# One engine for the output's copy, fewer maxima beside it, and a fourth maximum in an MLP's bursts: a transformer block on one core

## The chip, the core and the metric

The kernel runs on one core of a Trainium2 chip. The metric is the device time of one execution in microseconds (us). The core's engines are TensorE (PE; its weight loads are shown as PEld), VectorE (DVE), ScalarE (ACT), GpSimd (POOL) and SyncE (SP), which here issues every DMA. TensorE's results go to PSUM, of which there are eight banks of 128 x 512 fp32.

## The reference

```python
def _A_ref(x, wqkv, wo):                # S = 2048, D = 512
    H = 32; Dh = D // H                 # 32 heads of 16
    qkv = (x @ wqkv).reshape(B, S, 3, H, Dh).transpose(2, 0, 3, 1, 4)
    q, k, v = qkv[0], qkv[1], qkv[2]
    p = softmax(einsum("bhqd,bhkd->bhqk", q, k) * Dh ** -0.5)
    o = einsum("bhqk,bhkd->bhqd", p, v)
    return o.transpose(0, 2, 1, 3).reshape(B, S, D) @ wo

def _B_ref(x, w1, w2):                  # F = 1792
    return silu(x @ w1) @ w2

h = x + _A_ref(layernorm(x), wqkv, wo)
out = h + _B_ref(layernorm(h), w1, w2)
```

All is fp32; the weights of the MLP are scaled up by about 4.9.

## The kernel before

**Stages.** First the rows are normalized and projected to queries, keys and values. Then comes attention, in 32 *items*: an item is four heads for one block of 512 queries, so the eight items 8b to 8b+7 make up block b. An item has 16 *groups*, one for each 128 keys. Once the items of a block are done, its output projection is put beside groups 10 to 15 of the following item (`output`, in items 8, 16 and 24), and after that item the block's MLP runs (`finish_block`, `mlp`, at the group numbers in `marks`). Block 3 has its own ending (`finish_last`).

**A group** (main loop, numbers g; item i, group c): four score products (`scores`, tile `ps_s`, 64 rows of the array each), each followed on ScalarE by an exponential into `pt`; between them up to three maxima (`one_max`); and behind them the four value products of group g - 2 (`values`, tile `pv`, one bank for all items).

**Maxima.** The exponentials need each query's largest score beforehand. For that each item needs 64 *maxima* (`maximum`): a product of 48 rows into `ps_m`, on the other half of the array from the score before it, and a VectorE reduction of its 512 columns to `mx`. They are made ahead, for items up to four later. When the 64 of an item are complete, `finish_max` reduces them once more on VectorE and splits them on GpSimd (`ns`). Two steps later (`WAIT`) `place_max` transposes them on TensorE (`ps_n`), copies them (`mt`, on VectorE during attention) and places them by two DMAs into the query tile of their item. `maxima(g)` says how many a group gets, from a planner's rate with the maxima in the MLPs (`BESIDE`) taken off.

**Banks.** In attention and the MLPs one bank is `pv`, three (kind "sm") turn between maxima and their transposition, and four (kind "st") between scores, projections and the MLP's four sums `acc`.

**The end of an item.** After the values of its last group, which stand behind the scores of the next item's group 1, `finish_item` copies `pv` to `pvs`, the first half on ScalarE and the second on VectorE, and DMAs carry it on. The next item's values, behind group 2, overwrite `pv` and so come after both copies.

**An MLP** has 14 steps (`FC`). In each the first product (12 matmuls, into `pv`; in step 0 another bank) goes through `gate` (SiLU and a rounding on ScalarE, a subtraction `gl` on VectorE), and then the step before's second product (`second`, 12 matmuls to `ps_acc`) follows. `weave` puts bursts of three maxima behind the matmuls of given numbers: 4 and 12 of the first product and 8 of the second, or 4 and 10 of both in the steps of `EXTRA`. Each engine's instructions keep the order in which they are written down, since all are recorded with `keep_in_program_order`.

Of the kernel before, what the change touches and what calls it, by code (L numbers as in the profile page):

```python
# [10 lines left out]
F32 = mybir.dt.float32  # L11
# [9 lines left out]
P = 128  # L21
# [5 lines left out]
DC = D // P  # L27
FC = F // P
# [17 lines left out]
HEADS = [(0, 1), (0, 0), (1, 1), (1, 0)]  # L46
ITEMS = NB * H // 4

WAIT = 2
AHEAD = 4  # L50


BESIDE = (132, 132, 117)
OUTPUT = 9

BESIDE_A = (6,), 6

BESIDE_C = {3: ((4, 12), (8,)), 4: ((4, 10), (4, 10))}
BURST = 3

EXTRA = (4, 8), (6,), ()

QUIET = FC, FC, FC - 1


@with_exitstack
def attention_mlp_kernel(ctx: ExitStack, tc: tile.TileContext, x, wqkv, wo, w1, w2, out):
# [59 lines left out]
    def bank(name, kind="st", dtype=F32):  # L127
        return banks[kind].tile([P, 512], dtype, tag=kind, name=name)
# [73 lines left out]

    mx, left = {}, {}

    def maximum(i, kb, qt, a, j):
# [4 lines left out]
        ps = bank("ps_m", "sm")  # L210
        mm(ps, qs[i % RING][64 * j:64 * j + 48, a, qt * P:qt * P + P],
           ks[i % RING][64 * j:64 * j + 48, a, kb * 512:kb * 512 + 512], start=True, stop=True)
        pin(nc.vector.tensor_reduce(mx[i][:, j, a, qt, kb:kb + 1], ps, axis=AX.X, op=ALU.max))  # L213
        left[i] -= 1
        return left[i] == 0
# [34 lines left out]
    at = {"item": 0, "done": 0, "half": 0, "step": 0, "due": 0, "attention": False}  # L250
    agenda = {}

    def soon(steps, fn, *a):
# [10 lines left out]
            at["item"] += 1  # L264
        return at["item"]

    def one_max(half=None):
# [9 lines left out]
        if maximum(*todo[i, half].pop(0)):  # L277
            soon(WAIT, place_max, i, finish_max(i))

    def burst(n):  # L280
        for _ in range(n):
            one_max()

    def weave(steps, places, n=BURST):

        for k, _ in enumerate(steps):
            if k + 1 in places:
                burst(n)


    with ExitStack() as pa:
# [53 lines left out]
        def project_qk(b, n, beside=((), 0), scale=False):  # L345
# [4 lines left out]
            weave(product(ps, lambda c: wqk_h[:, c, cols], lambda c: wqk_l[:, c, cols],  # L350
                          lambda c: xth[b][:, c, :], lambda c: xtl[b][:, c, :], DC), *beside)
# [93 lines left out]
        for g in range(1, NG // 2):  # L445
            for m, (b, key) in enumerate([(b, 1) for b in range(NB)] + [(b, 0) for b in range(NB)]):
                tick()
                if g == 1 and m < 2:
                    fixed_rows(2 + m)

                n = 8 * g + m - 12
                project_qk(b, 2 * g + key, BESIDE_A if n < 19 else ((), 0), True)
# [16 lines left out]
    groups = ITEMS * KC  # L469
    pts, den = {}, {}  # L470

    def scores(g, k):

        i, c = divmod(g, KC)
        a, j = HEADS[k]
        assert i in placed
        ps = bank("ps_s")
# [20 lines left out]
    def finish_item(i):  # L498

        b, u = divmod(i, 8)  # L500
        pvs = bp.tile([P, 512], F32, name="pvs", bufs=1)
        act("copy", pvs[:, :256], pv[:, :256])
        dve("tensor_copy", pvs[:, 256:], pv[:, 256:])
        if i == ITEMS - 1:
            last.append(pvs)
            return
        dma(dn[i], pvs.rearrange("(k r) n -> k r n", r=32)[:, DH, :])
        for k in range(4):
            dma(ot[b % 2][place(i, k), :, u // 2, :], pvs[32 * k:32 * k + 16, :].rearrange("d (t n) -> d t n", n=P))
# [103 lines left out]
        low(gl, g, gh)  # L613
        return gh, gl

    def second(b, acc, f, gh, gl, places):
        w2h, w2l = ws.pop(("w2", f))
        while f == 0 and len(acc) < 4:
            acc.append(bank("ps_acc"))
        steps = (product(acc[t], lambda c: gh[:, t * P:(t + 1) * P], lambda c: gl[:, t * P:(t + 1) * P],  # L620
                         lambda c: w2h, lambda c: w2l, 1, start=f == 0, stop=f == FC - 1) for t in range(4))
        if f < FC - 1:
            weave(chain.from_iterable(steps), places)
            return
        for t, step in enumerate(steps):
            run(step)
            n = 4 * b + t
            h = rows_of(b, t)
            dve("tensor_tensor", h, acc[t], h, ALU.add)
            dma(out[n * P:(n + 1) * P, :], h)  # L630

    def mlp(b):

        first = bank("ps_w1")
        acc = [bank("ps_acc") for _ in range(3)]
        waiting = None
        for f in range(FC):
            tick()
# [9 lines left out]
            weave(product(ps, lambda c: w1h[:, c, :], lambda c: w1l[:, c, :],  # L648
                          lambda c: hth[:, c, :], lambda c: htl[:, c, :], DC), places[0])
            parts = gate(ps)  # L650
            if waiting:
                second(b, acc, *waiting, places[1])
# [35 lines left out]
    def finish_last(pending):  # L688
# [94 lines left out]
        for f in range(FC):  # L783
# [11 lines left out]
            if f:  # L795
                split_weights("w2", f - 1, "dve")
            if f > 1:
                second(b, acc, *waiting.pop(0), ())
        split_weights("w2", FC - 1, "dve")
        while waiting:  # L800
            second(b, acc, *waiting.pop(0), ())

    marks = [KC * (8 * b + 1) for b in range(1, NB)]

    def maxima(g):
# [18 lines left out]
    for g in range(groups):  # L824
        tick()
        i, c = divmod(g, KC)
        if g in marks:
# [7 lines left out]
        if i in (8, 16, 24):  # L835
            b, n = i // 8 - 1, c - OUTPUT
            if c < 4:
                load_rows(b, c)
# [14 lines left out]
                    soon(5, split_weights, "w1", f, "dve", "dve")  # L853
        if g == 1:
            dve("memset", pv, 0.0)
        n = maxima(g)
# [5 lines left out]
        if i in (8, 16, 24) and c > OUTPUT:  # L862
# [37 lines left out]
```

## Time and profile before

| | |
|---|---|
| median of 3 runs | 1729.4 us (1729.32 to 1729.89) |
| the profiled execution's own time | 1728.78 us |
| its span | 1727.0 us |
| TensorE busy | 1683.9 us (98%) |
| VectorE busy | 1460.4 us (85%) |
| ScalarE busy | 1247.6 us (72%) |
| granted TensorE clock, mean | 0.994 |

The span runs from the first to the last instruction that was recorded, and the execution's own time is 1.8 us longer. Matmuls are pipelined, so that a busy TensorE is not one at its peak, and TensorE's waits are read from the starts of its instructions. In the timeline each row has the start (us), the length (us), the engine, the line, the operation, output and input tiles with their shapes and the count of merged instructions; in brackets the idle time before it and what ended it. In the waits each row has who waited for whom, the total (us), how often, and the longest. In the table by stretches the columns are the stretch, its length, busy time and count of PE, PEld, DVE, ACT and POOL, the granted TensorE clock, the DMA share and GB/s. In the page's groups: line, engine, operation, tiles and shapes, count, busy time (us), mean of one (ns), idle time before them and what ended it.

### The profile page before, as it was taken

How to read it: one execution, taken by the hardware profiler on the slowest of the kernel's cores; microseconds unless marked ns; L12 is line 12 of the kernel's file. 1: busy time of each engine (PE TensorE's matmuls, PEld its weight loads, DVE VectorE, ACT ScalarE, POOL GpSimd, SP SyncE). 2: the span in 40 equal slices, each digit the busy share in tenths (PEclk: the TensorE clock that was granted, in tenths of full speed). 3: DMA queues.
4: the chain of work that ended last, by engine and by line, in shares of the span. 5: the costliest groups of instructions: out<-in, count | busy, mean ns of one | idle time of the engine just before them, and what ended most of it. 6: DMA issues, size and time to landing. Idle time of an engine off the chain costs nothing.

```text
span 1727.0 us, 28338 instructions
## 1 busy us (share of the span) xinstructions
PE 1683.9 (98%) x10498; PEld 648.1 (38%) x10498; DVE 1460.4 (85%) x2459; ACT 1247.6 (72%) x2465; POOL 233.0 (13%) x318
## 2 busy tenths in 40 slices
PE   6999999999999999999999999999999999999999
PEld 5656422222245532222245542222235542222377
DVE  6899899999978889999978889999978789997343
ACT  5223599999963269999963359999973369999743
POOL 2113300000032310000033310000023310000000
PEclk9999999999999999999999999999999999999999
DMA  6334311121222111111222211111122211100122
GB/s 186 101 80 152 112 35 37 36 48 38 62 70 77 56 48 31 36 42 44 59 59 79 67 40 32 40 38 44 53 70 80 68 34 45 34 11 20 56 80 80
DMA packets 100570, 102.81 MB, mean 60 GB/s; under 512 B 19028, under 2 KB 77204, under 8 KB 100432
## 3 DMA queue, kind: packets, MB, share of 16 engines
q1 hardware_dynamic: 100432, 101.01, 19.8%
q8 instruction: 82, 1.34, 0.3%
q14 instruction: 56, 0.46, 0.1%
HBM read 77.72 MB, written 17.29 MB: 55 GB/s over the span
## 4 chain that ended last, share of the span: by engine, by line
PE 58%; ACT 35%; DVE 4%; DMA 2%; issue 1%; SPq 0%; ACTq 0%; POOL 0%; POOLq 0%; DVEq 0%
ACT pt L88 33%; PE pv L74 19%; PE ps_acc L74 9%; PE ps_m L74 8%; PE ps_s L74 8%; PE ps_qk L74 5%; PE ps_wo L74 3%; PE ps_w L74 3%; DVE mx L213 2%; PE ps_v L74 2%; PE ps_tr L77 1%; DVE ot L91 1%; DMA va<-in_A_wqkv_dram 1%; DMA ks<-kd 1%; DVE pvs L91 1%
## 5 line engine op out<-in xcount | busy, mean ns | idle before, releaser
L213 DVE TENSOR_REDUCE mx<-ps_m 128x1 f32<-128x512 f32 x2048 | 1281.1, 682 | 108.5 <-PE ps_m L74 80.1
L88 ACT ACTIVATE pt<-ps_s 128x512 f32<-128x512 f32 x2048 | 1019.6, 616 | 41.1 <-PE ps_m L74 37.8
L74 PE MATMUL ps_s<-qs,ks 64*128 64x512 f16 x2048 | 550.6, 382 | 4.3 <-ACT pt L88 1.5
L74 PE MATMUL pv<-pt,va 128*17 128x512 f32 x4096 | 540.4, 601 | 6.3 <-DVE pvs L91 6.2
L74 PE MATMUL ps_m<-ks,qs 48*128 48x512 f16 x2048 | 527.7, 382 | 7.3 <-DVE mx L213 5.7
L74 PEld LDWEIGHTS <-ks 64*128 64x128 f16 x2048 | 153.9, 95 | 568.0 <-issue 458.3
L74 PEld LDWEIGHTS pv<-pt,va 128*17 128x17 f32 x4096 | 68.8, 95 | 233.8 <-issue 213.1
L74 PEld LDWEIGHTS <-qs 48*128 48x128 f16 x2048 | 122.8, 94 | 66.8 <-issue 63.1
L88 ACT CAST w2h<-w 128x512 fp32r<-128x512 f32 x56 | 34.7, 619 | 105.5 <-PE ps_acc L74 105.5
L88 ACT ACTIVATE g<-pv 128x512 f32<-128x512 f32 x39 | 23.3, 597 | 105.2 <-PE pv L74 105.2
L81 POOL TENSOR_SCALAR nm<-nm 128x16 f32<-128x16 f32 x32 | 8.3, 259 | 666.4 <-DVE nm L220 666.4
L74 PE MATMUL ps_acc<-w2h,gh 128*128 128x512 f32 x224 | 92.0, 411 | 0.0
L74 PE MATMUL ps_acc<-w2l,gh 128*128 128x512 f32 x224 | 91.3, 408 | 0.0
L74 PE MATMUL ps_acc<-w2h,gl 128*128 128x512 f32 x224 | 88.9, 397 | 0.0
L91 DVE TENSOR_TENSOR gl<-g,gh 128x512 fp32r<-128x512 f32 x56 | 40.2, 717 | 49.9 <-ACT gh L88 49.9
L81 POOL TENSOR_TENSOR w2l<-w,w2h 128x512 fp32r<-128x512 f32 x42 | 53.6, 1277 | 180.2 <-ACT w2h L88 180.2
L74 PE MATMUL pv<-hth,w1l 128*128 128x512 f32 x156 | 65.9, 423 | 0.0
L81 POOL TENSOR_TENSOR ot<-ot,den 128x512 f32<-128x512 f32 (+1 forms) x16 | 20.4, 1275 | 331.0 <-DMA den<-dr 292.8
L74 PE MATMUL pv<-hth,w1h 128*128 128x512 f32 x156 | 62.4, 400 | 0.0
L74 PE MATMUL pv<-htl,w1h 128*128 128x512 f32 x156 | 61.5, 394 | 0.0
L88 ACT ACTIVATE ks<-ps_qk,qk_s 128x512 f32<-128x512 f32 x24 | 16.5, 689 | 61.8 <-PE ps_qk L74 61.8
L81 POOL TENSOR_TENSOR w1l<-w,w1h 128x512 fp32r<-128x512 f32 x42 | 55.2, 1315 | 22.9 <-ACT w1h L88 22.9
(118 smaller groups left out, 1278.0 us busy)
## 6 DMA issues: line engine op xcount, KB each, us to landing
w<-in_B_w_dram SPq DMA_DIRECT2D x112, 256.0 KB
ks<-kd SPq DMA_DIRECT2D x120, 192.0 KB
qs<-qd SPq DMA_DIRECT2D x128, 48.0 KB
kd<-sh SPq DMA_DIRECT2D x16, 256.0 KB
qd<-sh SPq DMA_DIRECT2D x16, 256.0 KB
hx<-in_A_x_dram SPq DMA_DIRECT2D x16, 256.0 KB
out_dram<-ot SPq DMA_DIRECT2D x16, 256.0 KB
ot<-pvs SPq DMA_DIRECT2D x124, 32.0 KB
```

Of the source, the lines that this page charges most:

```text
L74: tc.keep_in_program_order(nc.tensor.matmul(*a, **k))
L77: tc.keep_in_program_order(nc.tensor.transpose(*a))
L81: tc.keep_in_program_order(getattr(nc.gpsimd, op)(*a, **k))
L88: pin(getattr(nc.scalar, fn)(*a, **k))
L91: pin(getattr(nc.vector, fn)(*a, **k))
L213: pin(nc.vector.tensor_reduce(mx[i][:, j, a, qt, kb:kb + 1], ps, axis=AX.X, op=ALU.max))
```

## The change

- The output's copy (`finish_item`) is no longer split. VectorE copies all of it; in items 8, 16 and 24, whose copy stands at the head of an MLP, ScalarE does; the last item keeps the halves.
- Group 2 of an item finds at most two maxima instead of three (`JOINT`, in `maxima`), save for items 0 to 2 and the items after an MLP.
- The transposition of an item's maxima is put off to the next group 2 (`due_at`), where that is early enough and no MLP has just run.
- In an MLP the burst in the second product (the second one in an `EXTRA` step) is of four; the first of these goes to `pv`. There are three, two and no `EXTRA` steps instead of two, one and none, and the third MLP's bursts end one step earlier (`QUIET`).
- Groups 10 to 13 of items 8, 16 and 24 find up to four maxima, with `BESIDE` counting 141, 138 and 112 in the MLPs.
- Eight scores of the two groups after an MLP are made inside its last two second products, in the banks of the maxima (`some_scores`), with the load of the exponential's table moved ahead; these two groups find no maxima instead of four each.
- Ahead of attention the last projection of queries and keys gets a burst of four.

```diff
-BESIDE = (132, 132, 117)
+BESIDE = (141, 138, 112)
...
-BESIDE_A = (6,), 6
-BESIDE_C = {3: ((4, 12), (8,)), 4: ((4, 10), (4, 10))}
-BURST = 3
-EXTRA = (4, 8), (6,), ()
-QUIET = FC, FC, FC - 1
+BESIDE_A = {6: 6}, {4: 4}
+BESIDE_C = ({4: 3, 12: 3}, {8: 4}), ({4: 3, 10: 3}, {4: 3, 10: 4})
+EXTRA = (4, 7, 10), (4, 8), ()
+QUIET = FC, FC, FC - 2
...
+    def due_at(i):
+        g = at["group"]
+        if g is None:
+            return WAIT
+        joint = g + WAIT + (JOINT - g - WAIT) % KC
+        return joint - g if joint < KC * i - 2 and joint // KC - 1 not in (-1, *FIRSTS) else WAIT
...
-            soon(WAIT, place_max, i, finish_max(i))
+            soon(due_at(i), place_max, i, finish_max(i))
...
-        act("copy", pvs[:, :256], pv[:, :256])
-        dve("tensor_copy", pvs[:, 256:], pv[:, 256:])
+        if i == ITEMS - 1:
+            act("copy", pvs[:, :256], pv[:, :256])
+            dve("tensor_copy", pvs[:, 256:], pv[:, 256:])
+        elif i in FIRSTS:
+            act("copy", pvs, pv)
+        else:
+            dve("tensor_copy", pvs, pv)
...
+        ahead = [(g, m ^ (g % 2)) for g in marks[b:b + 1] + [marks[b] + 1] for m in range(4)]
+        def some_scores(n):
+            for _ in range(n):
+                scores(*ahead.pop(0), "sm")
...
-            places = BESIDE_C[4 if f in EXTRA[b] else 3] if f < QUIET[b] else ((), ())
+            beside_1, beside_2 = BESIDE_C[f in EXTRA[b]] if f < QUIET[b] else ({}, {})
+            beside_1 = {k: (lambda n=n: burst(n)) for k, n in beside_1.items()}
+            beside_2 = {k: (lambda n=n: burst(n, *[pv] * (n == 4))) for k, n in beside_2.items()}
+            if f == FC - 1:
+                beside_2 = {8: lambda: some_scores(3)}
...
+            if f == FC - 1:
+                act("activation", small.tile([P, 1], F32, name="sw"), ident[:, :1], AF.Exp)
...
-        act("activation", small.tile([P, 1], F32, name="sw"), ident[:, :1], AF.Exp)
-        second(b, acc, *waiting, ())
+        second(b, acc, *waiting, {2: lambda: some_scores(3), 8: lambda: some_scores(2)})
...
-        if g < LAG + 3 or g in marks or g - 1 in marks:
-            at["due"] = 0
+        if g < LAG + 3:
+            at["due"] = 1
             return 4
-        n = max(0, min(3, int(at["due"]), ready - at["done"]))
+        if g in marks or g - 1 in marks:
+            return 0
+        most = 2 if c == JOINT and i > 2 and i - 1 not in FIRSTS else 4 if i in FIRSTS and OUTPUT < c < OUTPUT + 5 else 3
+        n = max(0, min(most, int(at["due"]), ready - at["done"]))
...
-            scores(g, k)
+            if (g, k) not in pts:
+                scores(g, k)
```

More of the change, by code (lines that the diff above doesn't have):

```diff
@@ L47 @@
 ITEMS = NB * H // 4
+FIRSTS = 8, 16, 24
 WAIT = 2
+JOINT = 2
 AHEAD = 4
-BESIDE = (132, 132, 117)
+BESIDE = (141, 138, 112)
 OUTPUT = 9
-BESIDE_A = (6,), 6
-BESIDE_C = {3: ((4, 12), (8,)), 4: ((4, 10), (4, 10))}
-BURST = 3
-EXTRA = (4, 8), (6,), ()
-QUIET = FC, FC, FC - 1
+BESIDE_A = {6: 6}, {4: 4}
+BESIDE_C = ({4: 3, 12: 3}, {8: 4}), ({4: 3, 10: 3}, {4: 3, 10: 4})
+EXTRA = (4, 7, 10), (4, 8), ()
+QUIET = FC, FC, FC - 2
 @with_exitstack
@@ L203, in attention_mlp_kernel, with maximum @@
     mx, left = {}, {}
-    def maximum(i, kb, qt, a, j):
+    def maximum(i, kb, qt, a, j, ps=None):
         if i not in mx:
@@ L209, in maximum @@
             left[i] = 64
-        ps = bank("ps_m", "sm")
+        if ps is None:
+            ps = bank("ps_m", "sm")
         mm(ps, qs[i % RING][64 * j:64 * j + 48, a, qt * P:qt * P + P],
@@ L249, in attention_mlp_kernel @@
     END = 64 * ITEMS
-    at = {"item": 0, "done": 0, "half": 0, "step": 0, "due": 0, "attention": False}
+    at = {"item": 0, "done": 0, "half": 0, "step": 0, "due": 0, "attention": False, "group": None}
     agenda = {}
@@ L265, in next_item, with one_max @@
         return at["item"]
-    def one_max(half=None):
+    def due_at(i):
[4 more added lines that the diff above has]
+        return joint - g if joint < KC * i - 2 and joint // KC - 1 not in (-1, *FIRSTS) else WAIT
+    def one_max(half=None, ps=None):
         i = next_item()
@@ L276, in one_max, with burst, weave @@
         at["done"] += 1
-        if maximum(*todo[i, half].pop(0)):
-            soon(WAIT, place_max, i, finish_max(i))
-    def burst(n):
-        for _ in range(n):
+        if maximum(*todo[i, half].pop(0), ps):
+            soon(due_at(i), place_max, i, finish_max(i))
+    def burst(n, *more):
+        for ps in more:
+            one_max(ps=ps)
+        for _ in range(n - len(more)):
             one_max()
-    def weave(steps, places, n=BURST):
+    def weave(steps, inserts):
         for k, _ in enumerate(steps):
-            if k + 1 in places:
-                burst(n)
+            if k + 1 in inserts:
+                inserts[k + 1]()
     with ExitStack() as pa:
@@ L343, in measure, with project_qk @@
             pin(nc.scalar.reg_load(qk_f, qk_e[:1, :].bitcast(U32)))
-        def project_qk(b, n, beside=((), 0), scale=False):
+        def project_qk(b, n, beside={}, scale=False):
             g, key = divmod(n, 2)
@@ L350, in project_qk @@
             weave(product(ps, lambda c: wqk_h[:, c, cols], lambda c: wqk_l[:, c, cols],
-                          lambda c: xth[b][:, c, :], lambda c: xtl[b][:, c, :], DC), *beside)
+                          lambda c: xth[b][:, c, :], lambda c: xtl[b][:, c, :], DC),
+                  {k: (lambda n=n: burst(n)) for k, n in beside.items()})
             sh = xp.tile([P, 512], F16, name="sh")
@@ L451, in attention_mlp_kernel @@
                 n = 8 * g + m - 12
-                project_qk(b, 2 * g + key, BESIDE_A if n < 19 else ((), 0), True)
+                project_qk(b, 2 * g + key, BESIDE_A[n == 19], True)
                 if 0 <= n < 8:
@@ L470, in attention_mlp_kernel, with scores @@
     pts, den = {}, {}
-    def scores(g, k):
+    def scores(g, k, kind="st"):
         i, c = divmod(g, KC)
@@ L476, in scores @@
         assert i in placed
-        ps = bank("ps_s")
+        ps = bank("ps_s", kind)
         mm(ps, ks[i % RING][64 * j:64 * j + 64, a, c * P:(c + 1) * P], qs[i % RING][64 * j:64 * j + 64, a, :],
@@ L614, in gate, with second @@
         return gh, gl
-    def second(b, acc, f, gh, gl, places):
+    def second(b, acc, f, gh, gl, inserts={}):
         w2h, w2l = ws.pop(("w2", f))
@@ L622, in second @@
         if f < FC - 1:
-            weave(chain.from_iterable(steps), places)
+            weave(chain.from_iterable(steps), inserts)
             return
         for t, step in enumerate(steps):
-            run(step)
+            weave(step, {k - 3 * t: fn for k, fn in inserts.items()})
             n = 4 * b + t
@@ L648, in mlp @@
             weave(product(ps, lambda c: w1h[:, c, :], lambda c: w1l[:, c, :],
-                          lambda c: hth[:, c, :], lambda c: htl[:, c, :], DC), places[0])
+                          lambda c: hth[:, c, :], lambda c: htl[:, c, :], DC), beside_1)
             parts = gate(ps)
+            if f == FC - 1:
+                act("activation", small.tile([P, 1], F32, name="sw"), ident[:, :1], AF.Exp)
             if waiting:
-                second(b, acc, *waiting, places[1])
+                second(b, acc, *waiting, beside_2)
             waiting = f, *parts
-        act("activation", small.tile([P, 1], F32, name="sw"), ident[:, :1], AF.Exp)
-        second(b, acc, *waiting, ())
+        second(b, acc, *waiting, {2: lambda: some_scores(3), 8: lambda: some_scores(2)})
     found = {}
@@ L797, in finish_last @@
             if f > 1:
-                second(b, acc, *waiting.pop(0), ())
+                second(b, acc, *waiting.pop(0))
         split_weights("w2", FC - 1, "dve")
         while waiting:
-            second(b, acc, *waiting.pop(0), ())
+            second(b, acc, *waiting.pop(0))
     marks = [KC * (8 * b + 1) for b in range(1, NB)]
@@ L826, in attention_mlp_kernel @@
         i, c = divmod(g, KC)
+        at["group"] = None
         if g in marks:
@@ L834, in attention_mlp_kernel @@
             soon(8, split_wo, g, w)
-        if i in (8, 16, 24):
+        if i in FIRSTS:
             b, n = i // 8 - 1, c - OUTPUT
@@ L855, in attention_mlp_kernel @@
             dve("memset", pv, 0.0)
+        at["group"] = g
         n = maxima(g)
@@ L858, in attention_mlp_kernel @@
             k = m ^ (g % 2)
-            scores(g, k)
+            if (g, k) not in pts:
+                scores(g, k)
             if m < n:
                 one_max(1 - HEADS[k][1])
-        if i in (8, 16, 24) and c > OUTPUT:
+        if i in FIRSTS and c > OUTPUT:
             output(i // 8 - 1, c - OUTPUT - 1)
```

## The prediction

> **What bounds the kernel now.** I read the page first, then the waits, then the timeline of one item's boundary, of an MLP and of the stretches before and after an MLP.
>
> ```profile
> span 1727.0 us, 28338 instructions
> ...
> PE 1683.9 (98%) x10498; PEld 648.1 (38%) x10498; DVE 1460.4 (85%) x2459; ACT 1247.6 (72%) x2465; POOL 233.0 (13%) x318
> ...
> L213 DVE TENSOR_REDUCE mx<-ps_m 128x1 f32<-128x512 f32 x2048 | 1281.1, 682 | 108.5 <-PE ps_m L74 80.1
> ```
>
> TensorE is busy 98% of the span, so almost nothing is to be had but TensorE's own waits. The wait that the change is about is that for the output's copy, which ScalarE and VectorE share by halves:
>
> ```profile
> DVE pvs L91 <- ACT pvs L88: 35.3, 30, 11.3
> ```
>
> VectorE waits for ScalarE's half (30 times, 35.3 us in all), and TensorE, as the next rows show, for VectorE's. One boundary in the timeline (groups 1 to 3 of item 12), the engines in order of time:
>
> ```profile
> 724.29 1.89 DVE L213 TENSOR_REDUCE mx<-ps_m 128x1 f32<-128x512 f32 x3
> ...
> 724.81 1.05 PE L74 MATMUL pv<-pt,va 128*17 128x512 f32 x8
> 725.79 0.39 PE L74 MATMUL ps_s<-qs,ks 64*128 64x512 f16 x1
> ...
> 726.18 0.40 ACT L88 COPY pvs<-pv 128x256 f32<-128x256 f32 x1
> ...
> 726.62 0.42 DVE L91 COPY pvs<-pv 128x256 f32<-128x256 f32 x1 [0.44 <-ACT pvs L88]
> 726.96 3.67 DVE L213 TENSOR_REDUCE mx<-ps_m 128x1 f32<-128x512 f32 x6
> ...
> 727.10 1.05 PE L74 MATMUL pv<-pt,va 128*17 128x512 f32 x8 [0.26 <-DVE pvs L91]
> ...
> 728.08 0.39 PE L74 MATMUL ps_s<-qs,ks 64*128 64x512 f16 x1
> ...
> 728.89 0.37 PE L74 MATMUL ps_m<-ks,qs 48*128 48x512 f16 x1
> ...
> 729.41 1.05 PE L74 MATMUL pv<-pt,va 128*17 128x512 f32 x8
> ...
> 730.39 0.39 PE L74 MATMUL ps_s<-qs,ks 64*128 64x512 f16 x1
> ```
>
> An undisturbed group takes TensorE 0.98 us from its first score to its values (725.79 less 724.81 is the other half, also 0.98): 1.96 us, with three maxima beside the scores at no cost. Two losses stand here. The values of the new item start at 727.10 and not at 725.79 + 0.98 = 726.77: 0.32 us for the copy. Then VectorE is behind by its 0.44 of idling and 0.42 of copying, the third maximum of the next group waits for one of three banks, and the values come 1.33 us after the score (728.08 to 729.41) where 0.98 would do: 0.35 us. Together 0.68 us for each boundary. Seven items (1 to 7) and six (10 to 15) lie between these pairs of first scores:
>
> ```profile
> 232.18 0.39 PE L74 MATMUL ps_s<-qs,ks 64*128 64x512 f16 x1
> ...
> 458.39 0.39 PE L74 MATMUL ps_s<-qs,ks 64*128 64x512 f16 x1
> ...
> 657.41 0.39 PE L74 MATMUL ps_s<-qs,ks 64*128 64x512 f16 x1
> ...
> 850.84 0.39 PE L74 MATMUL ps_s<-qs,ks 64*128 64x512 f16 x1
> ```
>
> 226.21 us for 112 groups is 6.7 above 112 x 1.96, and 193.43 for 96 groups is 5.3 above: 12.0 in 13 items, 0.92 each, of which 0.68 is the boundary and 0.24 the transposition of the maxima wherever it falls, with the reduction before it.
>
> **Part 1, the boundary: the copy moves to VectorE whole, and the third group finds two maxima.** A whole 128x512 output from PSUM is taken at the reduction's 0.68 us (same size and source); the half's row, 0.42, and its double, 0.84, are the bounds. VectorE's third maximum of the second group ends at 724.29 + 1.89 = 726.18, and the next instruction can start some 0.08 before that, as 726.96 does before the copy's end at 727.04. The last values were done at 725.86, so nothing holds the copy: 726.10 to 726.78. TensorE starts 0.06 after a copy's end (727.04 to 727.10): 726.84 instead of 726.77, a loss of 0.07. Behind the copy stand on VectorE the maxima's small copy, where a transposition is joined, and two maxima:
>
> ```profile
> L91 DVE COPY mt<-ps_n x29: 149/202/213, 239.2 to 1588.6; 32x128 f16<-32x128 f16 x29
> ```
>
> With steps of 0.60 (six in 3.67) they end at about 726.70 + 0.13 + 1.20 = 728.03, before the next group's first maximum can be ready (score at 727.83, + 0.4). So VectorE is back in step, and the 0.35 goes too. What is late next is TensorE's own 1.96. The transposition takes a fourth bank turn in that group and so delays its second maximum by 0.17, but the third is gone, and its 0.22 slot covers that; without this cover it would cost 0.17 x 13. ScalarE is rid of 0.40 at each boundary; TensorE sets the pace, so nothing is counted for that. Gain: 0.68 - 0.07 = 0.61 at each of 25 boundaries, 15.3. Items 1 and 2 keep three maxima and gain 0.26 each; item 31 has no maxima and gains 0.3 by the copy alone: 0.8 together. In the built order the transposition is joined with the copy in 13 items; of their 0.24 I take 0.09, since the reduction stays: 1.2 (bounds 0 and 3.1). **Sum: -17.3 us** (with the copy at 0.84: 0.23 lost instead of 0.07, -13).
>
> **Part 2, the scores ahead under an MLP's end.** Eight scores and exponentials move in front of the end, and the two groups after an MLP find no maxima. The four groups after each MLP, up to the first steady one:
>
> ```profile
> 622.44 0.39 PE L74 MATMUL ps_s<-qs,ks 64*128 64x512 f16 x1
> ...
> 633.89 0.39 PE L74 MATMUL ps_s<-qs,ks 64*128 64x512 f16 x1
> ...
> 1013.88 0.39 PE L74 MATMUL ps_s<-qs,ks 64*128 64x512 f16 x1
> ...
> 1025.87 0.39 PE L74 MATMUL ps_s<-qs,ks 64*128 64x512 f16 x1
> ...
> 1401.36 0.39 PE L74 MATMUL ps_s<-qs,ks 64*128 64x512 f16 x1
> ...
> 1409.86 0.39 PE L74 MATMUL ps_s<-qs,ks 64*128 64x512 f16 x1
> ```
>
> They take 11.45, 11.99 and 8.50 us, 31.9 in all, with eight maxima queued on VectorE behind the last output additions. Part of the first is a slow TensorE:
>
> ```profile
> 626.00:631.10 5.10, 5.09 (x18) 0.60 (x19) 3.63 (x7) 3.27 (x6) 0.19 (x1) 0.50 0.01 2
> ```
>
> The granted clock is 0.50 there. Changed, two of the four groups are done beforehand, and the others take 1.96 each and 0.2 for the fourth score, which waits for the last addition's bank: 4.1 x 3 = 12.3. The five scores in the last product cost 0.62 (three, as a burst of three does in part 4: 0.53 from 532.01 to 532.54, and 0.09 of changing over) and 0.4 (two, an estimate: one turn of 0.22 less): 3.1 for three MLPs. The three in the product before replace a burst in the first two and are new (0.62) in the third, which also loses a burst sequence of three (3 x 0.62). Their exponentials are behind a table load either way. **Sum: -31.9 + 12.3 + 3.1 + 0.6 - 1.9 = -17.8 us.** Bounds: 1.0 worse for each MLP if the scores wait for their banks.
>
> **Part 3, four maxima beside an output projection.** Groups 10 to 13 of items 8, 16 and 24 go from three maxima to four, and there are three banks, so the fourth waits until VectorE has read the first, and the projection behind it on TensorE waits too:
>
> ```profile
> 485.47 1.25 DVE L213 TENSOR_REDUCE mx<-ps_m 128x1 f32<-128x512 f32 x2
> ...
> 485.81 0.50 PE L74 MATMUL ps_wo<-wo_h,oh 128*128 128x512 f32 x1
> ...
> 490.86 0.50 PE L74 MATMUL ps_wo<-wo_h,oh 128*128 128x512 f32 x1
> 490.95 1.88 DVE L213 TENSOR_REDUCE mx<-ps_m 128x1 f32<-128x512 f32 x3
> ```
>
> VectorE begins so late because the row addition and statistics stand ahead. Group 12: first maximum read at 490.95 + 0.68, fourth from 491.69, projection 0.31 later at 492.0 instead of 490.86: 1.13. Group 11 by the same steps 0.68, group 13 between them, 0.8; in group 10 the fourth is read before a score bank is free, for which the projection waits anyway. **Sum: +2.6 x 3 = +7.8 us** (bounds 0, and 1.13 in all twelve, 13.6).
>
> **Part 4, the fourth maximum in the MLP.** The burst in the second product goes from three to four, the added one into the idle output bank; it runs beside the third, on the other half of the rows, so TensorE's 0.62 for a burst stays. VectorE needs one step more before the next burst:
>
> ```profile
> 529.86 1.89 DVE L213 TENSOR_REDUCE mx<-ps_m 128x1 f32<-128x512 f32 x3
> ...
> 532.01 0.60 PE L74 MATMUL ps_m<-ks,qs 48*128 48x512 f16 x3
> ...
> 532.54 0.50 PE L74 MATMUL pv<-hth,w1l 128*128 128x512 f32 x1
> ```
>
> Four end at 529.86 + 1.89 + 0.60 = 532.35; the next burst's third (532.24, 0.3 before the product goes on at 532.54) wants the last one's bank, and starts at 532.40: 0.16 lost, in 30 ordinary steps, +4.8 (bounds 0 and, with one whole step of 0.60, 18). The output bank itself is read first, by 530.55, before the next product at 531.00. A step with a fourth burst costs
>
> ```profile
> 563.46 0.40 PE L74 MATMUL pv<-hth,w1h 128*128 128x512 f32 x1
> ...
> 571.23 0.40 PE L74 MATMUL pv<-hth,w1h 128*128 128x512 f32 x1
> ...
> 580.63 0.50 PE L74 MATMUL pv<-hth,w1h 128*128 128x512 f32 x1
> ```
>
> 9.40 instead of 7.77, and there are two more of them: +3.3. **Sum: +8.1 us.**
>
> **Part 5, small.** Four maxima in the last projection before attention cost TensorE a burst's 0.62; their 2.4 on VectorE lie in this idle time of 3.41:
>
> ```profile
> 197.12 1.29 DVE L213 TENSOR_REDUCE mx<-ps_m 128x1 f32<-128x512 f32 x2 [3.41 <-PE ps_m L74]
> ```
>
> One maximum more in the sixth group, where VectorE is behind, is estimated at most of a step, 0.5. The last transposition stands two groups ahead of its item instead of three: 0.4, an estimate, if its DMA lands late. **+1.5 us.** Other moved DMAs (the two that place each item's maxima) pass none that a score waits for soon.
>
> **Sum.** -17.3 - 17.8 + 7.8 + 8.1 + 1.5 = -17.7. The profiled execution took 1728.8 (span 1727.0); its median stands 0.6 higher. 1728.8 - 17.7 + 0.6 gives 1711.7 us.
>
> **Rivals.** *The boundary keeps its first wait* (0.13): VectorE's copy comes late because a reduction of finished maxima sits ahead, so that values still wait 0.32. 0.25 x 28 = 7.0 less: 1718.7. For it speaks that VectorE has only 0.1 to spare in a group; against, that the copy no longer waits for ScalarE.
>
> *The bank waits don't come* (0.11): parts 3 and 4's waits are hidden, 12.6 better: 1699. Against: the rows above show TensorE with no room.
>
> *The clock falls beside the projections* (0.07): TensorE now waits 0.7 to 1.1 three times in 16 us. The row at 0.50 shows that short waits can do it; one such stretch of 5.1 us at half clock costs 2.55, three 7.7: 1719.4. Against: the same stretch has waits now, and its clock is 1.00:
>
> ```profile
> 476.00:509.00 33.00, 31.06 (x193) 14.18 (x185) 24.32 (x43) 21.89 (x42) 10.08 (x13) 1.00 0.24 69
> ```
>  The Trainium skill (TensorE: Matmul & The Clock Gate, "A second HAM failure mode: psum-queue depth-cycling") says that frequent short idling between groups of matmuls makes the clock fall and rise; the row at 0.50 agrees, and by that rule this rival would be the case.
>
> *Slower: VectorE is held in the MLP* (0.10). One subtraction there took more than twice its usual time:
>
> ```profile
> 515.50 1.60 DVE L91 TENSOR_TENSOR gl<-g,gh 128x512 fp32r<-128x512 f32 x1
> ```
>
> It stood beside GpSimd's subtractions. If the extra step makes the two meet in each of the 35 steps that got a fourth maximum, VectorE is 0.92 later (1.60 - 0.68), and next bursts wait for it: +32, 1744. It decides from 0.51 a step (17.7 / 35). Against: an ordinary step has VectorE's subtraction 2 us after GpSimd's are over, and both move together. The Trainium skill (SBUF — State Buffer, "Who interferes with whom") says that a VectorE instruction with two SBUF inputs contends with GpSimd's reads, and a reduction or a copy out of PSUM does not; the 1.60 agrees, and by it the moved copy is safe.
>
> That the change doesn't do what it says can be read in the built order: the copies, joined transpositions, fours and early scores are there. So no chance is kept for it.
>
> **How the numbers follow.** My sum has 0.59 and, with its bounds, reaches from 1704 to 1719. The range 1700 to 1722 takes in the first and third rival and leaves out most of the second and the slow one. A measurement of this kernel tells 0.2%, 3.5 us, from no change. Faster by more: 0.59 + 0.13 + 0.11 + 0.05 = 0.88; slower: 0.09, most of the slow rival; same 0.03.
>
> **What would show it.** Right: 1.96 to 2.05 us for groups 1 to 3 of an ordinary item, no wait of VectorE for ScalarE's copy, two groups of 2 us after an MLP at clock 1.00, about 7.93 a step in the MLP, and TensorE waiting for maxima ahead of projections. Wrong: values waiting 0.3 for the copy, MLP steps over 8.3, or clock below 1 beside the projections.

## The result

The changed kernel takes 1718.49 us (median of 4 runs, 1717.20 to 1719.96); the kernel before took 1729.36 beside it (4 runs, 1729.25 to 1729.89). The ratio is 0.9937, 95% interval 0.9920 to 0.9954: 10.9 us faster, where 17.7 were forecast. The profiled execution is the fastest of the four, 1717.20 us, 1.3 below their median (0.6 in the kernel before); its span of 1715.4 is 11.6 below the one before.

Lines of the page after, and one row of its waits:

```profile
span 1715.4 us, 28218 instructions
...
PE 1673.1 (98%) x10498; PEld 645.6 (38%) x10498; DVE 1466.4 (85%) x2456; ACT 1239.8 (72%) x2437; POOL 233.3 (14%) x318
...
L217 DVE TENSOR_REDUCE mx<-ps_m 128x1 f32<-128x512 f32 x2013 | 1261.2, 684 | 89.4 <-PE ps_m L77 61.8
...
DVE pvs L94 <- ACT pvs L91: 12.0, 1, 12.0
```

TensorE is still the bound. VectorE's wait for ScalarE's half of the output is gone from 29 of its 30 places; the one left is the last item's. Since the changed kernel has the same 10498 matmuls, the difference is waiting, clock and which matmuls run beside each other. The table measures it between starts of first scores and first MLP products, in us, before and after; the groups that it leaves out (the fifth of items 9, 17 and 25 to their last) differ by less than 0.1:

| stretch | before | after | difference |
|---|---|---|---|
| up to item 1 (start, item 0) | 232.17 | 233.04 | +0.9 |
| items 1 to 7 | 226.21 | 224.39 | -1.8 |
| items 10 to 15 | 193.43 | 190.37 | -3.1 |
| items 18 to 23 | 193.30 | 190.28 | -3.0 |
| items 26 to 30 | 160.75 | 157.80 | -3.0 |
| items 8, 16, 24 up to their tenth group | 55.37 | 54.01 | -1.4 |
| from there to the MLP, three together | 98.34 | 106.51 | +8.2 |
| MLP, first product to the last chunk's, three | 302.48 | 308.01 | +5.5 |
| from there to the fifth group after the MLP, three | 61.52 | 47.79 | -13.7 |
| item 31 up to its sixteenth group | 29.73 | 29.44 | -0.3 |

**The boundary**, the same place in item 12 as the prediction shows it:

```profile
721.12 2.64 DVE L217 TENSOR_REDUCE mx<-ps_m 128x1 f32<-128x512 f32 x4
722.39 1.05 PE L77 MATMUL pv<-pt,va 128*17 128x512 f32 x8
...
723.41 0.39 PE L77 MATMUL ps_s<-qs,ks 64*128 64x512 f16 x1
723.68 0.68 DVE L94 COPY pvs<-pv 128x512 f32<-128x512 f32 x1
...
724.41 1.05 PE L77 MATMUL pv<-pt,va 128*17 128x512 f32 x8
725.40 0.39 PE L77 MATMUL ps_s<-qs,ks 64*128 64x512 f16 x1
...
727.36 0.39 PE L77 MATMUL ps_s<-qs,ks 64*128 64x512 f16 x1
```

The whole copy takes 0.68 us and follows VectorE's maxima without a gap; the values start 0.05 after its end. From score to score the groups are 1.99 and 1.96 us. The whole item takes 31.42 us instead of 32.04, and 16 x 1.96 is 31.36: the boundary now costs 0.06.

**Beside the projections and in the MLP** stand the new waits; first the timeline of item 8's group 12, with the clock of that stretch (the number before the last two), then one step of the MLP:

```profile
490.07 2.48 DVE L217 TENSOR_REDUCE mx<-ps_m 128x1 f32<-128x512 f32 x4
...
490.81 0.37 PE L77 MATMUL ps_m<-ks,qs 48*128 48x512 f16 x1 [0.86 <-DVE mx L217]
...
491.11 0.50 PE L77 MATMUL ps_wo<-wo_h,oh 128*128 128x512 f32 x1
...
476.00:511.00 35.00, 31.44 (x186) 14.63 (x186) 25.21 (x45) 20.86 (x41) 10.10 (x13) 1.00 0.21 62
```

```profile
531.88 0.39 PE L77 MATMUL pv<-hth,w1h 128*128 128x512 f32 x1
...
533.27 0.37 PE L77 MATMUL ps_m<-ks,qs 48*128 48x512 f16 x1
533.33 1.89 DVE L217 TENSOR_REDUCE mx<-ps_m 128x1 f32<-128x512 f32 x3
...
539.80 0.39 PE L77 MATMUL pv<-hth,w1h 128*128 128x512 f32 x1
```

TensorE idles 0.86 us before the fourth maximum, which wants the bank that VectorE reads first, and the projection starts 0.30 after that. Groups 11, 12 and 13 of item 8 are 0.67, 1.14 and 0.80 us longer than before (0.68, 1.13 and 0.8 forecast). In the MLP, the burst's third maximum is late (533.27), and the step takes 531.88 to 539.80, 7.92 us, where it was 7.77.

**After the MLP**, the last product, the joined transposition, the first score of the third group and of the fifth, and the clock:

```profile
627.88 0.40 PE L77 MATMUL ps_acc<-w2l,gh 128*128 128x512 f32 x1
628.20 0.23 PE L80 MATMUL ps_n<-ident_h,ns 128*32 128x128 f16 x1
628.37 0.39 PE L77 MATMUL ps_s<-qs,ks 64*128 64x512 f16 x1
...
632.64 0.39 PE L77 MATMUL ps_s<-qs,ks 64*128 64x512 f16 x1
...
622.00:634.00 12.00, 12.00 (x69) 4.66 (x71) 8.32 (x15) 10.02 (x20) 0.00 (x0) 1.00 0.27 97
```

Two groups in 4.27 us, and no time below full clock, where the kernel before had 5.1 us at 0.50. After the second MLP it had 0.72 over 12 us; after the third the clock was 1.00 in both kernels.

### The profile page after: what moved, and what is told of

It reads as the page before. It is cut to its first block, busy times and chain, and to the rows that moved or that the text cites. A ratio compares the mean times of both kernels' runs of the same rounds, so it can differ in the third digit from the quotient of the medians.

```text
span 1715.4 us, 28218 instructions
## 1 busy us (share of the span) xinstructions
PE 1673.1 (98%) x10498; PEld 645.6 (38%) x10498; DVE 1466.4 (85%) x2456; ACT 1239.8 (72%) x2437; POOL 233.3 (14%) x318
## 4 chain that ended last, share of the span: by engine, by line
PE 81%; ACT 8%; DVE 7%; issue 2%; DMA 1%; SPq 0%; POOL 0%; ACTq 0%; POOLq 0%; DVEq 0%
PE pv L77 31%; PE ps_s L77 19%; PE ps_m L77 10%; PE ps_acc L77 8%; ACT pt L91 6%; PE ps_qk L77 5%; DVE mx L217 5%; PE ps_w L77 3%; PE ps_v L77 2%; PE ps_wo L77 1%; PE ps_tr L80 1%; DMA va<-in_A_wqkv_dram 1%; DVE gl L94 1%; DVE ot L94 1%; SPq L97 0%
## 5 line engine op out<-in xcount | busy, mean ns | idle before, releaser
L217 DVE TENSOR_REDUCE mx<-ps_m 128x1 f32<-128x512 f32 x2013 | 1261.2, 684 | 89.4 <-PE ps_m L77 61.8
L77 PE MATMUL ps_s<-qs,ks 64*128 64x512 f16 x2048 | 538.5, 380 | 5.8 <-ACT pt L91 1.9
L77 PE MATMUL ps_m<-ks,qs 48*128 48x512 f16 x2013 | 520.0, 381 | 12.1 <-DVE mx L217 10.8
L77 PEld LDWEIGHTS <-ks 64*128 64x128 f16 x2048 | 149.7, 94 | 551.6 <-issue 443.6
L84 POOL TENSOR_TENSOR w1l<-w,w1h 128x512 fp32r<-128x512 f32 x42 | 55.6, 1323 | 13.9 <-ACT w1h L91 13.9
```

What stands on the lines that cost most here:

```text
L77: tc.keep_in_program_order(nc.tensor.matmul(*a, **k))
L84: tc.keep_in_program_order(getattr(nc.gpsimd, op)(*a, **k))
```

## The experiments

My theory: the boundary, the early scores, the fourth maxima beside projections and those in the MLP each do what the prediction said, and the gain that is missing went into what is left in the items (the reduction of an item's finished maxima and their transposition). The rivals: that the early scores give less because of the clock or their banks, that the joined transposition delays the groups it is put in, or that the parts are not independent. The kernel before was timed beside each run on the same chip: 1730.28 us for the first four runs below, 1729.81 for the later reduction in the kernel before and for the three edits together, 1728.66 for the others. The ratios are to these. The changed kernel was timed beside 1729.36 alone, so a difference from its 1718.49 carries about 1 us of chips.

**The boundary undone.** The copy is by halves again, the third group finds three maxima and the transposition comes two groups after the last maximum:

```diff
-            soon(due_at(i), place_max, i, finish_max(i))
+            soon(WAIT, place_max, i, finish_max(i))
...
+        act("copy", pvs[:, :256], pv[:, :256])
+        dve("tensor_copy", pvs[:, 256:], pv[:, 256:])
...
+        most = 4 if i in FIRSTS and OUTPUT < c < OUTPUT + 5 else 3
```

> The changed kernel with its boundary as before: the output's copy in halves on two engines, three maxima in group 2, the transposition two steps after the last maximum. By the sizes of the prediction the boundary is worth 17.3 us, so 1718.5 + 17.3 = 1735.8 us. By the stages of the two traces (items, groups 0 to 9 of items 8, 16 and 24, and item 31 are 12.5 us shorter together) it is worth 12.5, so 1731.0 us; then an ordinary item is back at some 32.0 us.

Measured: 1723.35 us (1722.45 to 1725.77; ratio 0.9965, 0.9954 to 0.9976), below both expectations. Its boundary has the old wait again, but its projection of group 12 has not the new one:

```profile
725.21 0.40 ACT L91 COPY pvs<-pv 128x256 f32<-128x256 f32 x1
...
725.64 0.42 DVE L94 COPY pvs<-pv 128x256 f32<-128x256 f32 x1 [0.44 <-ACT pvs L91]
...
726.12 1.05 PE L77 MATMUL pv<-pt,va 128*17 128x512 f32 x8 [0.26 <-DVE pvs L94]
```

```profile
492.42 0.50 PE L77 MATMUL ps_wo<-wo_h,oh 128*128 128x512 f32 x1
492.51 1.88 DVE L217 TENSOR_REDUCE mx<-ps_m 128x1 f32<-128x512 f32 x3
```

The items (1 to 31 without the projections and MLPs) are some 14 us longer than the changed kernel's, and the three stretches from the tenth group to the MLP are 7.9 shorter (98.63 against 106.51). With a third maximum back in nearly every third group the planner asks for three beside each projection, although four are allowed. So the fourth maxima there are not a part by themselves: they are where the maxima went that the third groups lost. Net, the boundary is worth 1723.35 - 1718.49 = 4.9 us (5.6 between the spans), not 17.

**No fourth maximum beside a projection**, and three instead of two again in the third groups, save in the items whose number leaves 0, 4 or 6 when divided by 8:

```diff
-        most = 2 if c == JOINT and i > 2 and i - 1 not in FIRSTS else 4 if i in FIRSTS and OUTPUT < c < OUTPUT + 5 else 3
+        most = 2 if c == JOINT and i > 2 and i % 8 in (0, 4, 6) else 3
```

> The changed kernel without the fourth maxima beside the output projections; their four per block go to group 2 of four of the items (three there instead of two). If the fourth makes the projection wait for a bank, 2.65 us come back for each block, 8.0 in all, and the twelve third maxima in group 2 cost 0.35 each, 4.2: 1714.7 us. If the projections are long for another reason, nothing comes back and the 4.2 are lost: 1722.7 us.

Measured: 1715.60 us (1715.06 to 1716.08; 0.9918, 0.9901 to 0.9934). The three stretches are back at 32.58, 33.21 and 32.63 us, 8.1 less; items 10 to 15, 18 to 23 and 26 to 30, in which 11 third groups have their third maximum back, take 5.6 more. That prices the exchange: a maximum costs about 0.51 us in a third group and 0.68 beside a projection (8.1 for 12). Group by group, the 0.51 is 0.35 in five items, as expected, and 0.66 in the six whose third group also has the transposition. The changed kernel pays it at the dearer place.

**The fourth maximum in the MLP reduced over 64 of its 512 columns** (the other 448 are left out; the matmul stays):

```diff
+        n = 512 if ps is None else 64
...
-        pin(nc.vector.tensor_reduce(mx[i][:, j, a, qt, kb:kb + 1], ps, axis=AX.X, op=ALU.max))
+        pin(nc.vector.tensor_reduce(mx[i][:, j, a, qt, kb:kb + 1], ps[:, :n], axis=AX.X, op=ALU.max))
```

> The changed kernel in which VectorE's reduction of the added maximum of an MLP's bursts reads 64 of its 512 columns (448 columns are left out); TensorE's work is the same. If the 0.16 us by which a step of the MLP is longer are VectorE's step, which makes the next burst wait for a bank, a step goes from 7.93 back to 7.77 us, 30 of them, 4.8 in all: 1713.7 us. If TensorE's own product costs them, nothing changes: 1718.5 us.

Measured: 1711.97 us (1710.49 to 1712.64; 0.9895, 0.9879 to 0.9912), 6.5 less than the changed kernel.

```profile
530.67 0.23 DVE L218 TENSOR_REDUCE mx<-pv 128x1 f32<-128x64 f32 x1
530.82 1.88 DVE L218 TENSOR_REDUCE mx<-ps_m 128x1 f32<-128x512 f32 x3
533.27 1.89 DVE L218 TENSOR_REDUCE mx<-ps_m 128x1 f32<-128x512 f32 x3 [0.58 <-PE ps_m L77]
```

VectorE, with 0.23 instead of 0.68 for the added one, is idle again when the next burst comes. The three MLPs are 5.5 us shorter, while TensorE does the same work: the fourth maximum costs VectorE's step, through the bank, not TensorE's turn.

**No scores ahead of the MLP's end**; the two groups after it still find no maxima. In the first two MLPs a burst of four maxima stands again where the first three of the scores were, so TensorE has no turn less there:

```diff
-            if f == FC - 1:
-                beside_2 = {8: lambda: some_scores(3)}
...
-        second(b, acc, *waiting, {2: lambda: some_scores(3), 8: lambda: some_scores(2)})
+        act("activation", small.tile([P, 1], F32, name="sw"), ident[:, :1], AF.Exp)
+        second(b, acc, *waiting)
```

> The changed kernel without the eight scores inside the end of each MLP, but still with no maxima in the two groups behind it. If the gain there is the early scores alone, it all goes: 15.6 us by the stages of the traces, 1734.1 us. If most of it is that VectorE has no maxima queued behind the last additions, the two groups now cost ScalarE's pace of 1.94 us each, less the places inside the MLP (1.05 for five scores and 0.62 for three): 2.1 for each MLP, 6.2 in all, 1724.7 us, with the clock at 1.00 behind the MLPs.

Measured: 1722.39 us (1721.05 to 1726.45; 0.9954, 0.9938 to 0.9971), 3.9 above the changed kernel. The profiled execution is the longest of its four. The start after its first MLP, and the clock a little later:

```profile
627.42 0.39 PE L77 MATMUL ps_acc<-w2l,gh 128*128 128x512 f32 x1
627.74 0.73 PE L77 MATMUL ps_s<-qs,ks 64*128 64x512 f16 x3
628.81 0.37 PE L77 MATMUL ps_s<-qs,ks 64*128 64x512 f16 x1 [0.34 <-ACT pt L91]
...
630.00:634.00 4.00, 3.67 (x17) 0.60 (x15) 1.92 (x3) 4.00 (x9) 0.00 (x0) 0.67 0.20 65
```

Here the scores stand together, the fourth waits 0.34 for ScalarE to free a bank, and the granted clock falls to 0.67 as it fell before the change, where the second expectation had 1.00. After the third MLP it stays at 1.00, with TensorE idle 1.0 of 6 us:

```profile
1404.00:1410.00 6.00, 4.99 (x28) 1.23 (x26) 2.66 (x6) 6.00 (x13) 0.68 (x3) 1.00 0.43 147
```

From the MLP's last chunk to the fifth group it takes 19.66, 19.61 and 16.12 us, between the kernel before (22.07, 22.60, 16.85) and the changed one (16.51, 16.51, 14.77). In these profiles 6.1 of the 13.7 us thus come from finding no maxima there, and 7.6 from the early scores, part of it clock. The medians give the early scores 3.9; since this profiled execution is 4.1 above its kernel's median, the 7.6 is an upper figure.

**The joining undone**: the transposition comes two groups after the last maximum, wherever that is.

```diff
-            soon(due_at(i), place_max, i, finish_max(i))
+            soon(WAIT, place_max, i, finish_max(i))
```

> The changed kernel whose transpositions all stand two steps after the last maximum; the copy on VectorE and the two maxima of group 2 stay. The prediction took 0.09 us for each of the 13 transpositions that are joined with the copy: 1718.5 + 1.2 = 1719.7 us. The trace after shows some 0.55 us lost in items with a separate transposition (14, 15, 22) and 0 to 0.3 in those with a joined one (11, 12, 13): 0.3 for each of 13, 1722.4 us.

Measured: 1717.85 us (1716.34 to 1720.54; 0.9939, 0.9922 to 0.9956): no difference. Items 10 to 15, 18 to 23 and 26 to 30 are longer by 0.8 us together (190.57, 190.49, 158.19), items 1 to 7 are shorter by as much, 0.6 of it by an earlier DMA ahead of item 8 (Part 5 below). Nine transpositions are joined in the 17 items, so the 0.8 is 0.09 each, as forecast; the medians can't show so little.

**The reduction of finished maxima one maximum later**: it is issued behind the next maximum, so that it doesn't read what was written right ahead of it.

```diff
+    def finish_ended():
+        j, at["ended"] = at["ended"], None
+        if j is not None:
+            soon(due_at(j), place_max, j, finish_max(j))
...
-        if maximum(*todo[i, half].pop(0), ps):
-            soon(due_at(i), place_max, i, finish_max(i))
+        ended = maximum(*todo[i, half].pop(0), ps)
+        finish_ended()
+        if ended:
+            at["ended"] = i
...
```

> The changed kernel in which the last reduction of an item's maxima (to nm) stands behind the next maximum on VectorE, and not right behind the one whose result it reads. In the trace after it starts 0.11 us after that one's end where others start 0.08 before it, so 0.19 us of some 0.3 are this wait. If what is left over in the items is VectorE's lost time around that reduction, 0.15 to 0.2 come back in each of 25 items: 4.4, 1714.1 us. If it is the reduction itself or the transposition, nothing: 1718.5 us.

Measured: 1713.82 us (1711.59 to 1714.65; 0.9914, 0.9898 to 0.9931), 4.7 less. In the timeline of item 14, first the changed kernel, then this one:

```profile
793.11 1.29 DVE L217 TENSOR_REDUCE mx<-ps_m 128x1 f32<-128x512 f32 x2 [0.26 <-PE ps_m L77]
794.51 0.22 DVE L224 TENSOR_REDUCE nm<-mx 128x16 f32<-128x64 f32 x1
794.65 2.47 DVE L217 TENSOR_REDUCE mx<-ps_m 128x1 f32<-128x512 f32 x4
```

```profile
789.95 1.89 DVE L217 TENSOR_REDUCE mx<-ps_m 128x1 f32<-128x512 f32 x3 [0.26 <-PE ps_m L77]
791.76 0.21 DVE L224 TENSOR_REDUCE nm<-mx 128x16 f32<-128x64 f32 x1
791.88 1.88 DVE L217 TENSOR_REDUCE mx<-ps_m 128x1 f32<-128x512 f32 x3
```

Directly behind the maximum it reads, the small reduction starts 0.11 after that one's end (794.40 to 794.51); with another in between, 0.08 before the end (791.76 against 791.84). VectorE gets 0.2 us back at each reduction. Items 10 to 15, 18 to 23 and 26 to 30 are 1.9 us shorter together, 0.11 each, and items 1 to 7 2.0, of which 0.8 is the DMA ahead of item 8.

**The same in the kernel before** (its burst, copy and planner untouched; the same edit, with its `WAIT` of two):

> The kernel before with the one edit that puts the last reduction of an item's maxima one maximum later. If what the reduction loses is its own wait for the result before it, as much comes back as in the changed kernel, some 4.7 us: 1724.7 us. If the losses at the boundaries of the kernel before left VectorE spare time that hid it, little comes back: 1728 us or more.

Measured: 1727.37 us (10 runs, 1726.05 to 1730.69; 0.9989, 0.9980 to 0.9999), 2.4 less by the medians, 1.9 by the ratio, whose interval reaches from 0.2 to 3.5. That looks like half of the 4.7, but in items 10 to 15, 18 to 23 and 26 to 30 the traces give 1.5 us here and 1.9 in the changed kernel. That the losses at the boundaries hid some of the delay is therefore not shown.

**The MLP's first burst one product later**, with the fourth maximum kept:

```diff
-BESIDE_C = ({4: 3, 12: 3}, {8: 4}), ({4: 3, 10: 3}, {4: 3, 10: 4})
+BESIDE_C = ({5: 3, 12: 3}, {8: 4}), ({4: 3, 10: 3}, {4: 3, 10: 4})
```

> The changed kernel with the first burst of an ordinary MLP step behind the fifth matmul of the first product instead of the fourth, so 0.23 us later; nothing is left out. If the fourth maximum costs its 0.16 us through the bank that this burst's third maximum waits for, the step goes from 7.93 to 7.77 us and 5.5 us come back (as the first stage of the run with the short fourth reduction showed): 1713.0 us. If the cost is VectorE's whole time in a step, the wait only moves to the next burst: 1718.5 us.

Measured: 1713.65 us (1711.92 to 1714.78; 0.9914, 0.9897 to 0.9930), 4.8 less.

```profile
531.76 0.39 PE L77 MATMUL pv<-hth,w1h 128*128 128x512 f32 x1
533.01 0.60 PE L77 MATMUL ps_m<-ks,qs 48*128 48x512 f16 x3
539.51 0.39 PE L77 MATMUL pv<-hth,w1h 128*128 128x512 f32 x1
```

The burst is whole (three in 0.60, none late), and the step is 7.75 us, no more than with three maxima. The fourth maximum in ordinary steps is free once VectorE has 0.23 us more before the next burst.

**The fourth maximum in the middle of a projection's products** (after six of its twelve, in the last three groups):

```diff
-            run(project_rows(n, ps))
+            weave(project_rows(n, ps), {6: one_max} if late else {})
...
+        late = n == 4 and i in FIRSTS and c > OUTPUT + 1
...
-            if m < n:
+            if m < min(n, 4 - late):
...
```

> The changed kernel whose fourth maxima in groups 11 to 13 stand in the middle of the projection's twelve products instead of ahead of them; the number of maxima is the same everywhere. If the fourth costs by waiting for the first one's bank (0.68, 1.13 and 0.8 us), it now costs its own place of 0.32 alone: 2.65 - 0.96 = 1.7 for each of three blocks, 5.1, 1713.4 us. If VectorE's time is the bound there, nothing comes back: 1718.5 us.

Measured: 1713.05 us, the median of 1712.28, 1712.53, 1713.56 and 2619.04; the last had a granted clock of 0.557, for a reason that isn't known, and the ratio of 0.9908 (0.9888 to 0.9928) is of the other three. That is 5.4 less, or 6.0 by the median of the three.

```profile
488.46 0.50 PE L77 MATMUL ps_wo<-wo_h,oh 128*128 128x512 f32 x1
...
490.05 0.39 PE L77 MATMUL ps_m<-ks,qs 48*128 48x512 f16 x1
490.36 0.51 PE L77 MATMUL ps_wo<-wo_h,oh 128*128 128x512 f32 x1
```

The projection of group 12 no longer waits; the fourth maximum goes in after six products. The three stretches take 34.11, 34.85 and 34.14 us, 3.4 less; the spans differ by 4.9, of which 0.8 is the DMA ahead of item 8.

**The last three edits of the changed kernel together** (reduction later, burst later, fourth maximum within the projection), with nothing left out:

> The changed kernel with three edits together, none of which leaves work out: the last reduction one maximum later, the first burst of an MLP step one matmul later, the fourth maxima in the middle of the projections. Alone they gave 4.7, 4.8 and 5.4 us. If each is a wait of TensorE at a place of its own, they add up: 1718.5 - 14.9 = 1703.6 us. If they draw on the same spare time of VectorE, less: 1707 to 1710 us.

Measured: 1704.59 us (1704.07 to 1706.48; 0.9857, 0.9840 to 0.9873): 25.2 us faster than the kernel before on its chip, 13.9 faster than the changed kernel, where the three gains add up to 14.9: within the chips' difference, the parts add up. It is the best version. One MLP step in it is 529.68 to 537.42, 7.74:

```profile
529.68 0.39 PE L77 MATMUL pv<-hth,w1h 128*128 128x512 f32 x1
...
537.42 0.39 PE L77 MATMUL pv<-hth,w1h 128*128 128x512 f32 x1
```

The boundary change alone on the kernel before was not tried, nor the changed kernel with three maxima in all bursts; whether all of an item's maxima would then be found in time is open.

## Why the prediction was right, and where it was off

The direction was right and 1718.49 lies in the range; the size was off by 6.8 us of 17.7, of which 6.1 are between the spans and 0.7 is where the profiled executions lie in their runs. By its own steps:

- **Part 1, -17.3, measured -13.5; the term that was mis-sized.** The boundary itself came as worked out: 0.06 lost in item 12, forecast 0.07, and the copy at the reduction's 0.68. What failed is the step "so VectorE is back in step" taken for the whole item, and with it the 0.24 that was to stay beside the boundary and even fall by 0.09 in 13 items. Between these two scores lie items 10 to 15:

```profile
656.16 0.39 PE L77 MATMUL ps_s<-qs,ks 64*128 64x512 f16 x1
...
846.52 0.39 PE L77 MATMUL ps_s<-qs,ks 64*128 64x512 f16 x1
```

 190.36 us less 96 x 1.96 leaves 2.2, of which 0.4 is six boundaries: 0.31 an item for the finished maxima's reduction and transposition. The same sum before gives 5.3 - 6 x 0.68 = 1.2, or 0.20 an item; over items 10 to 15, 18 to 23 and 26 to 30 it gives 0.16 before and 0.25 after. This loss was to fall by 1.2 us in all; instead it grew by about 0.1 an item, some 2.5 in 25 (an estimate). That is most of the 3.8. In the kernel before a reduction cost the groups around it 0 to 0.35 us, in the changed one 0 to 0.54 (items 14, 15 and 22). Running it one maximum later takes 0.09 an item off before and 0.11 after, so its late start explains little of the growth; the cause of the rest stays open.
- **Part 2, -17.8, measured -16.0** (13.7 after the MLPs, 2.2 of the last MLP's omitted bursts: its step without bursts takes 5.53 us instead of 7.77). Full clock and two short groups came as said. The slow clock stood after the first two MLPs alone, and they gained 5.6 and 6.1 us, the third 2.1. The first was to gain 6.3 (11.45 - 4.1 - 1.02). The shortfall is four small terms. The five scores of the last product cost 1.28 and not 1.02: its last 16 products take 5.15 us with them (623.05 to 628.20) and 3.87 before (618.57 to 622.44). By the 2.2, a burst too costs 0.75 and not 0.62. The transposition's product stands in front of the first score (628.20 to 628.37, 0.17) and was left out of the sum, the two groups took 4.27 instead of 4.1, and the last chunk's first product waits 0.2 for its burst's third maximum, the wait of Part 4.
- **Part 3, +7.8, measured +8.2.** Group 12's projection waits for the fourth maximum as worked out. Missed was why it is there at all: the boundary-undone run shows that these 8 us are the other side of Part 1, so that the two had to be priced as one exchange.
- **Part 4, +8.1, measured +7.8** (7.92 a step, 7.93 forecast; 5.5 and the 2.2 counted in Part 2). The short reduction shows it is VectorE's step.
- **Part 5, +1.5, measured +1.9**: 0.9 up to item 1, and 1.0 for a transposition whose DMA lands late. It is not the last one, for which 0.4 was allowed: nothing waits ahead of item 31. It is item 8's, which also moved from group 12 to 13 of the item before. In the other versions of the changed kernel this wait is 0 to 1.9 us, so its size here is partly chance:

```profile
457.43 0.39 PE L77 MATMUL ps_s<-qs,ks 64*128 64x512 f16 x1 [0.98 <-DMA qs<-mt]
```

Together -13.5 - 16.0 + 8.2 + 7.8 + 1.9 = -11.6, the difference of the spans.

**The rivals.** The boundary's first wait didn't stay, so 1718.7 was nearly met for a reason that is not that rival's: a reduction of finished maxima does delay VectorE, but anywhere in the item. The bank waits came in full. VectorE wasn't held in the MLP: 7.92 a step against the 8.3 that would have spoken for it. The clock didn't fall beside the projections: 1.00, although TensorE idled 3.6 of the 35 us shown. By the rule of the Trainium skill (TensorE: Matmul & The Clock Gate, "A second HAM failure mode: psum-queue depth-cycling") on frequent short idling it might have; this trace does not agree there, while the 0.50 and the 0.67 after the first MLP agree; after the third MLP, with TensorE idle 1.0 of 6 us and the clock at 1.00, it does not agree either. What separates these places stays open.

## What to carry to other kernels

When a schedule takes work out of one group, the same work has to be found a place in another: price the exchange, not the gain at the place it left (here 14 us at the boundaries for 8 beside the projections). When a schedule is tightened at one place, don't carry a small loss elsewhere over as a constant: what the reduction of finished maxima cost here depended on where it fell, and grew. And where a bank is what a new operation waits for, move the operation by one or two products before giving it up: two such moves, and one away from a result just written, brought 13.9 us more here.

## What the runs showed of the hardware

- A small reduction on VectorE right behind the reduction whose result it reads started 0.11 us after that one's end; with an independent one in between it started 0.08 before the end. The move was worth 4.7 us by the medians, and in 17 items in which it can be read group by group 0.11 us each.
- A whole 128x512 copy from PSUM takes VectorE 0.68 us, as much as a maximum over the same tile, where the half takes 0.42.
- After the first MLP, a wait of a third of a microsecond between scores went with a granted clock of 0.67 in 4 us behind it; with eight scores spread between the products before, the clock stayed at 1.00. After the third MLP it stayed at 1.00 even with TensorE idle 1.0 of 6 us.
